# Attention and SwiGLU kernel on one core: last block product in its own bank, another order of one-pair products, weight sums stored later and made sooner

## The chip, the cores and the metric

One Trainium2 chip, one core. The metric is the device time of one execution in microseconds (us); lower is better. A core has a matrix engine (TensorE, PE in the profile), a vector engine (VectorE, DVE), a scalar engine (ScalarE, ACT), GpSimd (POOL) and SyncE (SP), which here only issues DMAs. PE writes its results to PSUM, here eight banks of 128 x 512 float32; the other data lies in SBUF.

## The reference

Normed attention for 8 sequences, 12 heads, 448 tokens, head size 64; its output, 3584 x 768, goes through a feed-forward block with 1536 hidden units. All float32.

```python
q_n, k_n = rmsnorm(q, g_q), rmsnorm(k, g_k)
attn = softmax(q_n @ k_n.T / sqrt(64))
x = (attn @ v)  ->  (3584, 768)
xn = x / rms(x) * rms_g
g, val = xn @ w_gate, xn @ w_val            # 768 x 1536 each
out = (g * sigmoid(g) * val) @ w_out        # 1536 x 768
```

## The kernel before, in words

The program is laid out by hand: one Python function emits every instruction in a fixed order, and each engine works through its own list. `safe_scores` (the only part that runs on these inputs) goes through 48 pairs of heads. In between it pops items from a list `todo`: the gate and value products and the output products of the sequence before. A step is one call of `pe(fn)`; `now["t"]` counts them, and `after(n, fn)` emits `fn` n steps later.

**Products with fewer multiplications.** From sequence 1 on, gate and value use 15 products of block sums (`PRODUCTS`, `three`, `product`, matmuls on line 1408). The output product is a 2 x 2 block scheme with seven products, named after their right factors: B11, B21, T1 to T4, B22. The left factors are blocks A11 to A22 of the hidden values (tiles `h`) or their sums S1 to S4 (tiles `raw`). Three kinds of outputs:
- sequences 1 and 4, and 0 in plain form: `out_strassen` (matmuls on line 1681), two pairs of 128-row tiles for sequence 1, one pair for sequence 4. Each product takes two steps of three matmuls. B21 adds onto the bank of B11 and B22 onto that of T1, so the reader of the first must be done before the second starts. `ORDER_O` is the order.
- sequences 2, 3, 5, 6 and 7: `out_quads`, four tiles at once, where each of the seven products is itself split in the same way. `kept_q` holds the right factors of that second level. For each product i the steps are `a(i)`, `d(i-1)`, `bb(i)`, `c(i)`: a, b and c take two of the seven small products each, d the seventh, which adds onto c's bank. Matmuls on line 1752, left sums (tiles `l` and `raw`) on line 1626, DVE reads of the banks on lines 1772 to 1801; `finish` adds the results up on POOL (line 1723), for the last product on DVE (line 1743), and has `store` write them out (line 1578).

PE's results for this part go through three PSUM banks (`ps_f`), used in turn; scores use four others (`ps_s`).

**Weights.** All right factors lie in DRAM scratch (`kept`, `kept_o`, `kept_q`) and are streamed into an SBUF arena. `ask` (line 1287) issues a load as soon as the arena has a free place, in the order of use (`uses`); `used` gives a place back. All of it goes through SP's queue, together with the attention's inputs and the outputs.

**Weight sums for kept_q.** While sequence 1's outputs and sequence 2's gate and value products run, `derive_q` makes the second-level right factors: 21 jobs, each with two blocks x and y loaded from `kept_o` (line 1267), four DVE operations (lines 1371 to 1374) into two fresh places ta and tb, and four stores to `kept_q` (lines 1378 and 1381): a half of x, y, ta and tb. Two of these need no sum. `fill` calls `derive_q` after each step outside attention. A product of sequence 2's outputs may be loaded only when its three jobs are stored (`sums_q`).

Of the kernel before, what the change touches and what calls it, by code (L numbers as in the profile page):

```python
# [335 lines left out]
def safe_scores(  # L336
# [42 lines left out]
    def after(n, fn):  # L379
        due.append((now["t"] + n, fn))  # L380
# [562 lines left out]
    def norm_x(b):  # L943
# [293 lines left out]
    for b in range(1, B):  # L1237
        for n, g in enumerate(GROUPS):
            for at, name in enumerate(FIRST_RAWS if b == 1 else [right for _, _, right in PRODUCTS]):
                uses.append(("wg", b, g, name))  # L1240
        if in_quads(b):
            uses += stream_q(b)
        else:
            for name in ORDER_O:
                for c in range(NFP):
                    uses.append(("wo", b, name, c))
# [107 lines left out]
    todo_q = list(jobs_q)  # L1354

    def derive_q(wait=5):

        if not todo_q or sums_o or now["t"] - asked.get("at_q", 0) < 3 or asked["n"] in next_gate or not room(2, "wg"):
            return False
# [15 lines left out]

        def store():
            parts = kept_q[i].rearrange("p (n w) -> p n w", w=HW)
            nc.sync.dma_start(out=parts[:, j], in_=x[:, 0])
            for src, first, second in ((y, 1, 6), (ta, 2, 3), (tb, 4, 5)):
                gap = (second - first) * KG  # L1380
                nc.sync.dma_start(out=parts[:, first * KG + j:second * KG + j + 1:gap], in_=src)
# [181 lines left out]

    def store(b, n, i, y):
        row0 = at = b * S + i * 128 - 64 * (b % 2)
        while at < row0 + 128:
# [9 lines left out]
            else:  # L1576
                rows = out[rows + col:rows + col + m, cols]
            nc.sync.dma_start(out=rows, in_=y[at - row0:at - row0 + m, :])
            at += m
# [50 lines left out]
    def out_strassen(b):  # L1630
# [58 lines left out]
        pairs = out_pairs(b)  # L1689
        for name in ORDER_O:  # L1690
            for which in range(len(pairs)):
                for half in range(2):
                    steps.append(lambda a=(name, which, half, which == len(pairs) - 1): step(*a))
        return steps

    def out_quads(b):

        bank, dst, steps = {}, {}, []
        tiles = [i for pair in out_pairs(b) for i in pair]
        left = {}  # L1700
# [20 lines left out]
        def add(to, one, other):  # L1721
            for row in range(2):
                nc.gpsimd.tensor_tensor(to[row], one[row], other[row], ALU.add)  # L1723
# [50 lines left out]
        def bb(i):  # L1774
# [4 lines left out]
            nc.vector.tensor_tensor(u[:, 1], ps[:, 1], u[:, 0], ALU.add)  # L1779
            st["no_x"] = now["t"]  # L1780
            left_q1(b, i, (3,))
            if i == 0 or i > 1 and i + 1 < len(ORDER_Q):
                left_q1(b, i + 1, (0,))

        def c(i):
            ps = two(i, "c")
            st["heavy"] = now["t"]
            u3 = st["u", b, i][:, 1:2].to_broadcast([128, 2, HW])
            nc.vector.tensor_tensor(dst[i][1].rearrange("p (h n) -> p h n", h=2), ps, u3, ALU.add)
# [62 lines left out]
    def out_items(b):  # L1852
        if in_quads(b):
            return [(cost, TURNS, 0, fn) for cost, fn in out_quads(b)]
        if b >= FIRST_O:
            return [(NFP // 2 * HALF, TURNS, (0, ("wo", b, name, 3 * half + 2) if i == 0 else None), fn)
                    for (name, i, half), fn in zip(((name, i, half) for name in ORDER_O for i in range(len(out_pairs(b)))
                                                    for half in range(2)), out_strassen(b))]
# [180 lines left out]
    for g in range(NG + 1):  # L2039
# [62 lines left out]
        else:  # L2102
# [92 lines left out]
```

## Time and profile before

| | |
|---|---|
| median of 3 runs | 1487.42 us (1486.82 to 1487.74) |
| the profiled execution, own time | 1486.21 us |
| its span, first to last instruction | 1484.4 us |
| mean granted clock of TensorE | 0.997 |
| PE busy | 1456.5 us (98%) |
| DVE, ACT, POOL busy | 72%, 42%, 51% |
| last matmul ends | 1476.53 us |
| DMA queue of SP | 72.4% of 16 engines' span, 320.58 MB |

How to read it: times in the timeline are microseconds from the start of the span. A row is start, length, engine, line, operation, output <- inputs, shape and count; brackets give the idle time ahead of it and what ended it. SPq is SP's list of DMA issues. One fp32 matmul of the program shows as two in the trace, so a product of six shows x12.

### The profile page before, as it was taken

The numbers are of one execution on the slowest core, as the hardware profiler recorded it, in microseconds if no ns is written. First come the engines' busy times: TensorE is split into PE (matmuls) and PEld (weight loads), VectorE is DVE, ScalarE is ACT, GpSimd is POOL, SyncE is SP. The second block draws the span as 40 slices with busy tenths as digits, with TensorE's granted clock in tenths as the row PEclk, the third lists the DMA queues.
The fourth block names the chain that finished last, engine by engine and source line by source line (L and its number), as shares of the span: only waits on it lengthen the run. The fifth ranks groups of instructions, "written<-read, shape, count | busy, mean of one in ns | idle before, by whom it ended". The sixth has DMA issues, their size and how long they took to land.

```text
span 1484.4 us, 25739 instructions
## 1 busy us (share of the span) xinstructions
PE 1456.5 (98%) x8538; PEld 1141.9 (77%) x8538; DVE 1071.3 (72%) x1866; ACT 619.5 (42%) x1551; POOL 764.4 (51%) x684
## 2 busy tenths in 40 slices
PE   8999999999999999999999999999999999999997
PEld 4344444678855788888888889859898799899997
DVE  6788999699874677874579855755679756774664
ACT  7856776445523444234433443444542533101200
POOL 6877987647353363463545744645645842130002
PEclk9999999999999999999999999999999999999999
DMA  8758686676877899987566966677467855597675
GB/s 215 226 156 252 180 242 179 209 245 219 264 226 223 263 310 314 297 283 208 141 170 194 280 178 184 183 212 210 128 188 230 270 171 149 163 307 234 172 226 193
DMA packets 340577, 322.52 MB, mean 217 GB/s; under 512 B 126932, under 2 KB 282068, under 8 KB 340436
## 3 DMA queue, kind: packets, MB, share of 16 engines
q1 hardware_dynamic: 339508, 320.58, 72.4%
q8 instruction: 71, 1.16, 0.3%
q14 instruction: 70, 0.57, 0.1%
q10 hardware_dynamic: 800, 0.20, 0.1%
q0 software_dynamic: 128, 0.00, 0.0%
HBM read 266.90 MB, written 53.77 MB: 216 GB/s over the span
## 4 chain that ended last, share of the span: by engine, by line
PE 82%; DVE 11%; DMA 3%; issue 2%; SPq 1%; ACT 0%; POOL 0%; DVEq 0%; ACTq 0%; POOLq 0%
PE ff L1408 36%; PE ff L1752 13%; PE sc L805 8%; PE ff L1826 6%; PE av L823 6%; PE ff L1681 6%; PE ff L1551 2%; DMA w<-kept 2%; PE sc L705 1%; PE av L732 1%; PE den L749 1%; PE tr L684 1%; PE den L887 1%; DVE l L1626 1%; DVE x L959 1%
## 5 line engine op out<-in xcount | busy, mean ns | idle before, releaser
L909 POOL TENSOR_TENSOR es<-es,e 128x448 f32<-128x448 f32 x205 | 255.1, 1245 | 13.6
L1408 PE MATMUL ff<-x,w 128*128 128x224 f32 x1296 | 258.1, 353 | 0.3 <-DVE pc L1429 0.3
L1408 PEld LDWEIGHTS ff<-x,w 128*128 128x128 f32 x1296 | 243.6, 190 | 3.5 <-issue 2.1
L805 PE MATMUL sc<-qT,kT 64*64 64x448 f32 x1176 | 231.1, 539 | 0.0
L823 PE MATMUL av<-e,yard 64*64 64x448 f32 x1148 | 223.8, 538 | 0.0
L1408 PE MATMUL ff<-xs,w 128*128 128x224 f32 x832 | 164.7, 353 | 3.8 <-DMA w<-kept 3.1
L1408 PEld LDWEIGHTS ff<-xs,w 128*128 128x128 f32 x832 | 156.1, 190 | 7.7 <-issue 3.9
L805 PEld LDWEIGHTS sc<-qT,kT 64*64 64x64 f32 x1176 | 78.8, 133 | 86.1 <-issue 54.8
L786 POOL TENSOR_TENSOR ss<-ss,rd 128x448 f32<-128x448 f32 x40 | 47.6, 1191 | 159.4 <-ACT rd L785 158.0
L1752 PE MATMUL ff<-w,l 128*128 128x192 f32 x630 | 117.2, 329 | 4.5 <-DVE l L1626 2.2
L1429 DVE TENSOR_TENSOR pc<-ff,l 128x448 f32<-128x448 f32 x56 | 34.9, 622 | 108.6 <-PE ff L1408 77.8
L1826 PE MATMUL ff<-x,w 128*128 128x448 f32 x288 | 111.8, 541 | 0.0
L1752 PEld LDWEIGHTS ff<-w,l 128*128 128x128 f32 x630 | 103.8, 190 | 10.0 <-DVE l L1626 3.0
L823 PEld LDWEIGHTS av<-e,yard 64*64 64x64 f32 x1148 | 77.3, 133 | 36.9 <-issue 36.7
L904 POOL TENSOR_TENSOR es<-e 128x448 f32<-128x448 f32 x41 | 48.5, 1182 | 110.2 <-ACT e L813 79.9
L813 ACT ACTIVATE e<-sc 128x448 f32<-128x448 f32 x168 | 88.0, 547 | 36.5 <-PE sc L805 27.1
L1826 PEld LDWEIGHTS ff<-x,w 128*128 128x128 f32 x288 | 53.3, 190 | 51.1 <-issue 48.0
L811 ACT ACTIVATE e<-sc,yard 128x448 f32<-128x448 f32 x126 | 78.2, 634 | 32.7 <-PE sc L805 24.2
L1408 PE MATMUL ff<-top_x,w 128*128 128x224 f32 x440 | 91.1, 356 | 0.0
L1408 PEld LDWEIGHTS ff<-top_x,w 128*128 128x128 f32 x440 | 81.8, 190 | 11.5 <-issue 10.6
L1426 DVE TENSOR_TENSOR pb<-ff,pb 128x448 f32<-128x448 f32 x84 | 52.3, 622 | 47.8 <-PE ff L1408 47.7
L1723 POOL TENSOR_TENSOR y<-y,pa 128x384 f32<-128x384 f32 x10 | 11.1, 1127 | 144.6 <-DVE y L1801 137.2
(244 smaller groups left out, 2972.4 us busy)
## 6 DMA issues: line engine op xcount, KB each, us to landing
w<-kept SPq DMA_DIRECT2D x380, 256.0 KB, 3.9
w<-kept_q SPq DMA_DIRECT2D x350, 192.0 KB, 3.8
w<-kept_o SPq DMA_DIRECT2D x150, 192.0 KB, 3.8
kept_q<-w SPq DMA_DIRECT2D x63, 192.0 KB, 3.6
raw<-in_moe_w_gate_dram SPq DMA_DIRECT2D x24, 384.0 KB, 4.7
raw<-in_moe_w_val_dram SPq DMA_DIRECT2D x24, 384.0 KB, 4.2
kept<-w SPq DMA_DIRECT2D x48, 192.0 KB, 4.3
raw<-in_moe_w_out_dram SPq DMA_DIRECT2D x24, 384.0 KB, 3.7
```

The lines of the kernel that those rows point to most:

```text
L786: after(m, lambda: (nc.gpsimd.tensor_tensor(ss, ss, rd, ALU.add), st.update({("summed", b): hp})))
L805: nc.tensor.matmul(ps[r, 0:S], lhsT=keys(g, r, i), rhs=st["qT", g][r, :], start=True, stop=True)
L811: nc.scalar.activation(e, ps[:, 0:S], ACT.Exp, scale=st["rs", g][:, NB + i:NB + i + 1])
L813: nc.scalar.activation(e, ps[:, 0:S], ACT.Exp)
L823: nc.tensor.matmul(st["av", g][own(j), 0:S], lhsT=vt, rhs=st["e", g, i][r], start=i == 0, stop=i == PARTS - 1, skip_group_check=True)
L904: nc.gpsimd.tensor_tensor(st["es", g], st["e", g, 0], st["e", g, 1], ALU.add)
L909: nc.gpsimd.tensor_tensor(st["es", g], st["es", g], st["e", g, i], ALU.add)
L1408: nc.tensor.matmul(bank[:, w * HT:(w + 1) * HT], lhsT=data(key)[:, (2 * w + c) * 128:(2 * w + c + 1) * 128], rhs=a[left][:, c, :], start=o ...
L1426: nc.vector.tensor_tensor(T[name], ps[:, 0:S], T[name], ALU.add)
L1681: nc.tensor.matmul(ps, lhsT=left_o(b, which, LEFT_O[name], c), rhs=data(("wo", b, name, c)), start=first and c == 0, stop=c == NFP - 1, sk ...
L1752: nc.tensor.matmul(ps, lhsT=a[:, j, :], rhs=data(key)[:, n % 2 * HW:(n % 2 + 1) * HW], start=start and j == 0, stop=j == KG - 1, skip_grou ...
L1826: nc.tensor.matmul(bank[w][:, 0:S], lhsT=data(key)[:, c * 128:(c + 1) * 128], rhs=st["x", 0][:, 3 * half + c, :], start=half == c == 0, st ...
```

## The change

1. `norm_x`: the broadcast of the row scales of sequence 1 (`rb`) uses a bank of `ps_s` instead of `ps_f`.
2. `order_o`: outputs with one pair (sequence 4) run in the order B11, T2, B21, T3, T1, T4, B22 instead of B11, B21, T2, T3, T1, B22, T4. The weights are loaded in that order too.
3. `derive_q`: until the loads reach the first gate products of sequence 2, the fresh places are taken from the other end of the arena and a job may follow after 4 steps instead of 3; around the first seven of those loads jobs are allowed if three places are free, where none were before. The half of x and y are stored at once, ta and tb 3 steps later (before: all four 1 step later). ta, tb and y's places are given back 6 steps after the job (before: 7 for ta and tb, from the second product on). `derive_q` is also called once inside each attention block.
4. `out_quads` for the last sequence: the seventh small product of the last block product gets its own bank. Its left sum is made a product earlier. T1's result is added into tiles pb and pc by POOL row by row, and B22's small products are added to pb on the way, so no full-tile addition is left behind the last matmul; the two stores of the last tile go through SP's and ACT's queues.

The core of the diff:

```diff
-            ps = (ps_s if b > 1 else ps_f).tile([128, 512], F32, name="rb", tag="s" if b > 1 else "f")
+            ps = (ps_s if b else ps_f).tile([128, 512], F32, name="rb", tag="s" if b else "f")
...
     ORDER_O = ("B11", "B21", "T2", "T3", "T1", "B22", "T4")
+    def order_o(b):
+        return ORDER_O if len(out_pairs(b)) > 1 else ORDER
...
+    def own_kind():
+        return "w" if asked["n"] <= next_gate[0] else "wg"
     def derive_q(wait=5):
-        if not todo_q or sums_o or now["t"] - asked.get("at_q", 0) < 3 or asked["n"] in next_gate or not room(2, "wg"):
+        if not todo_q or sums_o or now["t"] - asked.get("at_q", 0) < (4 if asked["n"] <= next_gate[0] else 3) or asked["n"] in next_gate and not room(3, "wg") or not room(2, own_kind()):
             return False
...
-        st[own_a], st[own_b] = block("wg"), block("wg")
+        st[own_a], st[own_b] = block(own_kind()), block(own_kind())
...
-        def store():
-            parts = kept_q[i].rearrange("p (n w) -> p n w", w=HW)
-            nc.sync.dma_start(out=parts[:, j], in_=x[:, 0])
-            for src, first, second in ((y, 1, 6), (ta, 2, 3), (tb, 4, 5)):
-                gap = (second - first) * KG
-                nc.sync.dma_start(out=parts[:, first * KG + j:second * KG + j + 1:gap], in_=src)
+        def store(src, first, second):
+            gap = (second - first) * KG
+            nc.sync.dma_start(out=parts[:, first * KG + j:second * KG + j + 1:gap], in_=src)
+        def store_sums():
+            store(ta, 2, 3)
+            store(tb, 4, 5)
             asked["sums_q"] = asked.get("sums_q", 0) + 1
-        after(1, store)
+        nc.sync.dma_start(out=parts[:, j], in_=x[:, 0])
+        store(y, 1, 6)
+        after(3, store_sums)
         for key in (*keys, own_a, own_b):
-            after(7 if i and key[0] != "wx" else 4, lambda key=key: used(key))
+            after(6 if key[0] != "wx" else 4, lambda key=key: used(key))
...
+        end = len(ORDER_Q) - 1 if b == B - 1 else None
...
+        def split_sum(row):
+            m = dst[end - 1][row]
+            nc.gpsimd.tensor_tensor(dst[2][row], dst[2][row], m, ALU.add)
+            nc.gpsimd.tensor_tensor(dst[3][row], dst[3][row], m, ALU.add)
+            after(1, lambda: store(b, 1, tiles[2 + row], dst[3][row]))
         def finish(i):
-            if name == "B21":
+            if end and i == end - 1:
+                split_sum(0)
+                left_q1(b, end, (3,))
+                half = lo_hi(dst[end][0])[0]
+                nc.vector.tensor_tensor(half, half, lo_hi(dst[2][0])[0], ALU.add)
+            elif end and i == end:
+                store(b, 1, tiles[0], m[0], (nc.sync, nc.scalar))
+            elif name == "B21":
...
         def bb(i):
+            if end and i == end:
+                nc.vector.tensor_tensor(u[:, 0], u[:, 0], lo_hi(dst[2][0])[1], ALU.add)
+                both = dst[2][1].rearrange("p (h n) -> p h n", h=2)
+                nc.vector.tensor_tensor(both, both, u[:, 1:2].to_broadcast([128, 2, HW]), ALU.add)
+                return
...
         def c(i):
+            if end and i == end:
+                half = st["u", b, i][:, 0]
+                nc.vector.tensor_tensor(half, ps[:, 1], half, ALU.add)
+                nc.vector.tensor_tensor(dst[i][1].rearrange("p (h n) -> p h n", h=2), ps, dst[2][1].rearrange("p (h n) -> p h n", h=2), ALU.add)
+                store(b, 1, tiles[1], dst[i][1])
+                return
...
+            if end and i == end - 1:
+                split_sum(1)
         def d(i):
-            ps = bank[i, "c"]
-            term(i, 6, ps[:, 1], start=False)
+            if end and i == end:
+                ps = ps_f.tile([128, 512], F32, name="ff", tag="f")[:, 0:BW].rearrange("p (h n) -> p h n", h=2)
+            else:
+                ps = bank[i, "c"]
+            term(i, 6, ps[:, 1], start=bool(end) and i == end)
...
             pe(lambda: [step(g, i) for i in (1, 2)])
+            derive_q()
             pe(lambda: [step(g, i) for i in (3, 4)])
```

**SP's queue in the gate and value products of sequence 2, second group.** `w<-kept` loads a right factor, `w<-kept_o` a block for a later sum, `kept_q<-w` stores a part of a job. Before:

```order
L1287 DMA w<-kept 128x512
L1378 DMA kept_q<-w 128x192
L1381 DMA kept_q<-w 128x2x192 x3
L1287 DMA w<-kept 128x512
L1267 DMA w<-kept_o 128x384 x2
L1287 DMA w<-kept 128x512 x3
```

After, at the same place:

```order
L1290 DMA w<-kept 128x512
L1393 DMA kept_q<-w 128x192
L1386 DMA kept_q<-w 128x2x192
L1290 DMA w<-kept 128x512
L1270 DMA w<-kept_o 128x384 x2
L1386 DMA kept_q<-w 128x2x192 x2
L1290 DMA w<-kept 128x512 x4
```

The stores of ta and tb have moved behind one load of a right factor and two of blocks, and stand now directly ahead of the next right factors.

**PE in the outputs of sequence 4, between its first two attention blocks.** `h_115` to `h_118` are the hidden values (A11 and A12, or A22), `raw` the sums S2, S1 and S4. Before, from the second half of B21 on:

```order
L1681 MATMUL ff<-w,h_118 128x384 x3
L1681 MATMUL ff<-w,raw 128x384 x6
L1681 MATMUL ff<-w,h_115 128x384 x3
L1681 MATMUL ff<-w,h_116 128x384 x3
L1681 MATMUL ff<-w,raw 128x384 x12
L1681 MATMUL ff<-w,h_117 128x384 x3
```

After, from the second half of T2 on:

```order
L1693 MATMUL ff<-w,raw 128x384 x3
L1693 MATMUL ff<-w,h_117 128x384 x3
L1693 MATMUL ff<-w,h_118 128x384 x3
L1693 MATMUL ff<-w,h_115 128x384 x3
L1693 MATMUL ff<-w,h_116 128x384 x3
L1693 MATMUL ff<-w,raw 128x384 x6
L1693 MATMUL ff<-w,h_117 128x384 x3
L1693 MATMUL ff<-w,h_118 128x384 x3
L1693 MATMUL ff<-w,raw 128x384 x3
```

T2 stands ahead of B21, and T1 and B22, twelve matmuls in a row before, have T4 between them.

**DVE at the end.** Rows behind the last bank read of T1 (`pa`), up to the last one before the flag. `l` is a left sum, `th` a scratch tile, `ff` a bank, `y` an output tile. Before:

```order
L1801 TENSOR_TENSOR pa<-ff,th 128x192
L1778 TENSOR_TENSOR th<-ff,th 128x192
L1779 TENSOR_TENSOR th<-ff,th 128x192
L1626 TENSOR_TENSOR l_12385<-raw,l_12350 128x384
L1789 TENSOR_TENSOR y<-ff,th 128x384
L1801 TENSOR_TENSOR y<-ff,th 128x192
L1743 TENSOR_TENSOR y<-y,pa 128x384 x2
```

After:

```order
L1844 TENSOR_TENSOR pa<-ff,th 128x192
L1638 TENSOR_TENSOR l_12374<-raw,l_12350 128x384
L1750 TENSOR_TENSOR y<-y,pb 128x192
L1804 TENSOR_TENSOR th<-ff,th 128x192
L1805 TENSOR_TENSOR th<-ff,th 128x192
L1808 TENSOR_TENSOR th<-th,pb 128x192
L1810 TENSOR_TENSOR pb<-pb,th 128x384
L1821 TENSOR_TENSOR th<-ff,th 128x192
L1822 TENSOR_TENSOR y<-ff,pb 128x384
L1844 TENSOR_TENSOR y<-ff,th 128x192
```

The left sum has moved ahead of the reads of b's bank, the additions of T1's result stand ahead of the last three bank reads, and the last row is a bank read of 192 columns.

More of the change, by code (lines that the diff above doesn't have):

```diff
@@ L1243, in safe_scores @@
         else:
-            for name in ORDER_O:
+            for name in order_o(b):
                 for c in range(NFP):
@@ L1374, in derive_q @@
         nc.vector.tensor_tensor(tb[:, 0], y[:, 0], ta[:, 0], ALU.subtract)
-        def store():
-            parts = kept_q[i].rearrange("p (n w) -> p n w", w=HW)
-            nc.sync.dma_start(out=parts[:, j], in_=x[:, 0])
-            for src, first, second in ((y, 1, 6), (ta, 2, 3), (tb, 4, 5)):
-                gap = (second - first) * KG
-                nc.sync.dma_start(out=parts[:, first * KG + j:second * KG + j + 1:gap], in_=src)
+        parts = kept_q[i].rearrange("p (n w) -> p n w", w=HW)
+        def store(src, first, second):
[4 more added lines that the diff above has]
+            store(tb, 4, 5)
             asked["sums_q"] = asked.get("sums_q", 0) + 1
-        after(1, store)
+        nc.sync.dma_start(out=parts[:, j], in_=x[:, 0])
+        store(y, 1, 6)
+        after(3, store_sums)
         for key in (*keys, own_a, own_b):
-            after(7 if i and key[0] != "wx" else 4, lambda key=key: used(key))
+            after(6 if key[0] != "wx" else 4, lambda key=key: used(key))
         return True
@@ L1562, in project_out, with store @@
         store(b, n, i, y)
-    def store(b, n, i, y):
+    def store(b, n, i, y, queues=(nc.sync, nc.sync)):
+        queues = list(queues)
         row0 = at = b * S + i * 128 - 64 * (b % 2)
@@ L1577, in store @@
                 rows = out[rows + col:rows + col + m, cols]
-            nc.sync.dma_start(out=rows, in_=y[at - row0:at - row0 + m, :])
+            queues.pop(0).dma_start(out=rows, in_=y[at - row0:at - row0 + m, :])
             at += m
@@ L1689, in out_strassen @@
         pairs = out_pairs(b)
-        for name in ORDER_O:
+        for name in order_o(b):
             for which in range(len(pairs)):
@@ L1787, in c @@
             st["heavy"] = now["t"]
+            if end and i == end:
+                half = st["u", b, i][:, 0]
+                nc.vector.tensor_tensor(half, ps[:, 1], half, ALU.add)
+                nc.vector.tensor_tensor(dst[i][1].rearrange("p (h n) -> p h n", h=2), ps,
+                                        dst[2][1].rearrange("p (h n) -> p h n", h=2), ALU.add)
+                store(b, 1, tiles[1], dst[i][1])
+                return
             u3 = st["u", b, i][:, 1:2].to_broadcast([128, 2, HW])
@@ L1856, in out_items @@
             return [(NFP // 2 * HALF, TURNS, (0, ("wo", b, name, 3 * half + 2) if i == 0 else None), fn)
-                    for (name, i, half), fn in zip(((name, i, half) for name in ORDER_O for i in range(len(out_pairs(b)))
+                    for (name, i, half), fn in zip(((name, i, half) for name in order_o(b) for i in range(len(out_pairs(b)))
                                                     for half in range(2)), out_strassen(b))]
```

## The prediction

> **What bounds the kernel now.** I read the page first, then TensorE's (PE's) list of waits, then the places of those waits in the timeline, then the last 15 us.
>
> ```profile
> span 1484.4 us, 25739 instructions
> PE 1456.5 (98%) x8538; PEld 1141.9 (77%) x8538; DVE 1071.3 (72%) x1866; ACT 619.5 (42%) x1551; POOL 764.4 (51%) x684
> ```
>
> PE is busy for 1456.5 of 1484.4 us, so 27.9 us are idle. The change adds and removes no matmul, so it can win idle time and the stretch behind the last matmul, nothing else. The list of waits says which idle time the change can reach:
>
> ```profile
> PE ff L1408 <- DMA w<-kept: 3.1, 3, 1.8
> PE ff L1408 <- DVE pb L1426: 2.4, 4, 1.1
> ...
> PE ff L1752 <- DMA w<-kept_q: 1.0, 1, 1.0
> ...
> PE ff L1752 <- DVE y L1789: 0.7, 1, 0.7
> PE ff L1681 <- DVE y L1653: 0.7, 1, 0.7
> ...
> PE ff L1681 <- ACT pa L1660: 0.6, 1, 0.6
> ```
>
> Each row gives the total, the times and the longest wait. The first and the third row and one wait of the second belong to the stage in which the weight sums are made, the fourth row to the end, the last two to the one-pair outputs of sequence 4.
>
> **Weight sums (derive_q).** These are the five waits in that stage, in PE's timeline; the idle time ahead of the row stands in brackets:
>
> ```profile
> 510.36 1.75 PE L1408 MATMUL ff<-xs,w 128*128 128x224 f32 x8 [1.80 <-DMA w<-kept]
> 543.47 1.75 PE L1408 MATMUL ff<-xs,w 128*128 128x224 f32 x8 [0.50 <-DMA w<-kept]
> 573.59 1.75 PE L1408 MATMUL ff<-xs,w 128*128 128x224 f32 x8 [0.79 <-DMA w<-kept]
> 599.17 1.02 PE L1408 MATMUL ff<-raw,w 128*128 128x224 f32 x4 [0.81 <-DVE pb L1426]
> 607.52 0.92 PE L1752 MATMUL ff<-w,l 128*128 128x192 f32 x4 [0.96 <-DMA w<-kept_q]
> ```
>
> Together 4.86 us. The loads come late because they share SP's queue with the stores of the sums, and those wait for VectorE (DVE):
>
> ```profile
> SPq L1381 <- DVE w L1374: 24.4, 14, 5.1
> ...
> 501.30 2.23 SPq L1381 DMA_DIRECT2D kept_q<-w  x3
> ...
> 505.13 1.33 SPq L1287 DMA_DIRECT2D w<-kept  x3
> ...
> 566.55 3.97 SPq L1381 DMA_DIRECT2D kept_q<-w  x3
> ...
> 502.17 0.97 DVE L1374 TENSOR_TENSOR w<-w 128x192 f32<-128x192 f32 x1
> ```
>
> Three issues take 1.33, one 0.44; what the L1381 rows have above that, 0.9 and 2.6 us, is waiting with the loads queued behind. After the change the two stores that need no sum go out at once, and the two of sums three steps later instead of one; the number of DMAs is the same. At 510.36 (right factor b12 of the second group) the new order puts the stores of the sums right ahead of the load: they can go when L1374 ends at 503.14, take 0.9, so the load is issued near 504.1 instead of 505.13: 1.0 of the 1.80 goes. At 543.47 the queue ahead of the load is as long as before: 0.2 of 0.50. At 573.59 the load now stands ahead of the sums' stores, and the 2.6 us of waiting in front of it leave: all 0.79.
>
> The other two waits come from the last three of the 21 sums. The code's own step counter puts them at steps 366, 371 and 374 before and the last one at 357 after, so 12 DVE operations leave the stretch from 592 to 603 us. The first four took 3.16 us (592.17 to 595.33):
>
> ```profile
> 592.17 1.28 DVE L1371 TENSOR_TENSOR w<-w 128x192 f32<-128x192 f32 x1
> ...
> 594.97 0.36 DVE L1374 TENSOR_TENSOR w<-w 128x192 f32<-128x192 f32 x1
> ```
>
> That is more than the 0.81 that PE waited at 599.17, so this wait goes; and the loads of kept_q that were asked for 2 to 4 steps ahead of their use now get 7 to 12, so the 0.96 goes. Sum: 1.0 + 0.2 + 0.8 + 0.8 + 1.0 = **3.8 us**. Ends: all five go (4.86), or only the last two and half of the rest's 2.0 (2.8); worse is a rival below. The sums made instead during the outputs of sequence 1 cost nothing there: PE's timeline shows no wait between 408 and 476 us, and a bank comes back into use only two products of 4.0 us (the row at 980.65 below) after its own.
>
> The extra call of derive_q inside an attention block catches one sum. Four DVE operations at 0.35 to 1.28 us, 1.4 to 4.8 us together, stand ahead of the multiplication that frees the av bank, whose next user comes behind at least two products: nothing. If that cover is gone, PE waits for up to the remainder, under 2 us.
>
> **One-pair outputs (sequence 4).** Before, B21 adds to B11's bank right behind B11 and must wait until ACT has copied it; B22 adds to T1's bank right behind T1 and waits for DVE:
>
> ```profile
> 963.32 2.20 PE L1681 MATMUL ff<-w,h 128*128 128x384 f32 x6 [0.57 <-ACT pa L1660]
> 980.65 4.03 PE L1681 MATMUL ff<-w,raw 128*128 128x384 f32 x12
> 985.34 4.14 PE L1681 MATMUL ff<-w,raw 128*128 128x384 f32 x12 [0.65 <-DVE y L1653]
> ```
>
> Now T2 (row like 980.65, 4.0 us in another bank) stands between the first two and T4 between the second two; the readers need 0.5 us. Both waits go: **1.2 us**. T2 starts with the half of S2 that was made a stage earlier, so nothing new is late; if it were, the same 0.6 would come back.
>
> **The end (sequence 7, last product).** Timeline, engines mixed:
>
> ```profile
> 1466.51 0.55 DVE L1626 TENSOR_TENSOR l<-raw,l 128x384 f32<-128x384 f32 x1
> 1471.22 1.95 POOL L1723 TENSOR_TENSOR pc<-pc,pa 128x384 f32<-128x384 f32 x2 [4.88 <-DVE pa L1801]
> 1473.34 1.21 DVE L1626 TENSOR_TENSOR l<-raw,l 128x384 f32<-128x384 f32 x1
> 1473.44 1.14 PE L1752 MATMUL ff<-w,l 128*128 128x192 f32 x6
> 1474.67 0.56 DVE L1789 TENSOR_TENSOR y<-ff,th 128x384 f32<-128x384 f32 x1
> 1475.29 1.24 PE L1752 MATMUL ff<-w,l 128*128 128x192 f32 x6 [0.71 <-DVE y L1789]
> 1476.57 0.36 DVE L1801 TENSOR_TENSOR y<-ff,th 128x192 f32<-128x192 f32 x1 [1.34 <-PE ff L1752]
> 1477.03 1.03 DVE L1743 TENSOR_TENSOR y<-y,pa 128x384 f32<-128x384 f32 x2
> 1477.62 1.80 SPq L1578 DMA_DIRECT2D out_dram<-y  x3
> ```
>
> Before, the last six matmuls wait 0.71 for DVE to read the shared bank; then come 0.36 and 1.03 of DVE and three issues, ending at 1479.42. After, on the same clock: PE goes on at 1474.41 and ends near 1475.55. POOL gives the first row of pb near 1472.2 (half of 1.95 from 1471.22). DVE then has 0.36, twice 0.36, 0.36 and 0.55: done near 1474.4. Behind c's products (1474.58) it has 0.36 and 0.56, to 1475.6, and behind d's 0.36, to 1476.0. SP issues one store from 1475.6 and a half one from 1476.2, ending near 1476.75: 2.67 earlier.
>
> Is SP's end what counts?
>
> ```profile
> L2165 SPq EVENT_SEMAPHORE  x8: 17/17/17, 1482.3 to 1482.8; - x8
> ...
> L2165 ACTq EVENT_SEMAPHORE  x1: 17/17/17, 1473.2 to 1473.2; - x1
> ...
> L2164 ACTq TENSOR_LOAD <-flag x1: 480/480/480, 1469.8 to 1469.8; - x1
> ...
> 0.73 1.38 ACTq L560 DMA_DIRECT2D yard<-in_q_dram  x2
> ...
> DMA to landing us min/median/max: 2.2/2.3/2.5
> ```
>
> SP's last issue ends at 1479.42 and its last event is at 1482.8, 3.4 later; the span ends 1.6 behind that. The stores land 2.2 to 2.5 us after their issue (last row), which is sooner. ACT needs 3.4 us from its flag load to its event, and an issue on it takes 0.69 (1.38 for two). Its new half store goes from 1476.05 to 1476.74, so its event is near 1480.15; SP's, 3.4 behind 1476.75, as well. The end moves from 1482.8 to 1480.15, by 2.65. If DVE's operations with two SBUF inputs each lose a POOL operation, as at 1473.34 (1.21 for the 0.55 of 1466.51, so 0.66 more), and one such loss reaches the chain, it is 2.0. I take **2.5 us**, near the free case, since DVE has 0.2 us to spare ahead of c and the last three operations read PSUM.
>
> The Trainium skill, "SBUF — State Buffer", section "Who interferes with whom", says that a VectorE instruction with two SBUF inputs contends with a GpSimd instruction that reads SBUF, and that whoever comes second is blocked for the whole instruction. The row at 1473.34 agrees (1.21 against 0.55). By that rule at its worst two of POOL's operations are waited out whole, the sums ahead of c are ready near 1475.75 instead of 1474.4, and the end would win 1.6 instead of 2.5, which stays inside the forecast's own range.
>
> **rb in ps_s for sequence 1:** nothing. PE's timeline has no wait between 239 and 327 us, so none can go; a late bank could cost about what the longest wait on one does in the list, 0.7 us (L1789).
>
> **Sum.** 3.8 + 1.2 + 2.5 = 7.5 us. The profiled execution took 1486.21 (span 1484.4 and 1.8 around it), so 1478.7 by its own clock; it lies 1.21 below the median of the runs, 1487.42, so the forecast in those terms is 1479.9, with a range of its own from 1478.0 (4.86 + 1.2 + 2.65 = 8.7, and 0.7 of spread) to 1482.0 (2.8 + 1.2 + 2.0 = 6.0, less 0.6).
>
> **Rivals.**
> - *The queue stays the limit.* If SP's issue rate (near 567 us some ten issues of 0.44 us to three products of 1.75 us) and not the waiting makes the loads late, and DVE is late at 599 for its other work, the first stage gives 0 to 1.5: 1482.0 to 1484.3. For it: 543.47, whose queue is as long as before. Against it: 2.6 us of pure waiting at 566.55.
> - *The end is held by something else*, such as the reused y tile, whose previous store now stands behind one that waits for POOL: POOL starts on it at 1468.4, behind the first row below, and needs two operations of 0.98; the store goes near 1470.8, lands 2.5 us later, 1473.3, and is needed at 1475.0. It has 1.7 us to spare; if it failed, 1 to 2.5 us less, 1480.9 to 1482.4, within the other ranges.
> - *Slower: places.* Made sooner, the sums take places in the weight arena during the outputs of sequence 1, so eight later loads are asked for 6 to 8 steps ahead instead of 9 to 12. A load that comes late has cost up to 1.80 (510.36). At that price eight cost 14.4 against the 7.5: 1494.3. It decides once a lead of 6 steps, 12 us at half of 4.03 a step, is shorter than the way from issue to use, 5.1 us for the load of 505.13; it is twice as long, so I give it little.
>
> The rows for the last two, from the timeline and from the chain of work (start, length):
>
> ```profile
> 1467.79 0.56 DVE L1789 TENSOR_TENSOR pa<-ff,th 128x384 f32<-128x384 f32 x1 [0.26 <-PE ff L1752]
> ...
> 505.13 5.10 DMA w<-kept
> ```
>
> - *No effect:* new waits of the size of the old ones appear one step later: 1484.5 to 1490.4.
>
> **Chances.** Forecast 0.68; queue the limit 0.15; better than 1478.0 (waits that follow from these go too) 0.04; no effect 0.08; slower 0.05. A measurement of this kernel can tell about 0.2%, 3.0 us, from no change. So faster by more than that (below 1484.4): 0.87; within it 0.08; slower 0.05. The range reaches from 1477.2, the forecast's low end with some of the better case, to 1484.3, the end of the first rival.
>
> **What would show it.** Right: in the profile after, PE's waits for y L1653, pa L1660 and y L1789 are gone; no wait for w<-kept_q; w<-kept down to about 1 us; SP's wait on L1374 well below 24.4; the stretch from the last matmul to the end of the span 6.2 us instead of 7.9. Wrong: new PE waits for DMA between 408 and 520 us, SP still waiting over 10 us for the sums, or DVE operations of 1.2 us in the last 5 us.

## The result, and the profile after

| | before | after |
|---|---|---|
| median of 6 runs each, same chip | 1486.76 us (1484.12 to 1487.74) | 1475.10 us (1473.55 to 1476.27) |
| ratio, 95% interval | | 0.9924 [0.9911, 0.9936] |
| the profiled execution, own time | 1486.21 us | 1474.93 us |
| its span | 1484.4 us | 1473.1 us |
| PE idle in the span | 27.9 us | 19.2 us |

The forecast was 1479.9 us with a range from 1477.2 to 1484.3; the measured median lies below the range. The gain is 11.7 us by the medians and 11.3 by the spans, where 7.5 were forecast. The page of after:

```profile
span 1473.1 us, 25744 instructions
PE 1453.9 (99%) x8538; PEld 1142.2 (78%) x8538; DVE 1073.0 (73%) x1868; ACT 620.1 (42%) x1551; POOL 763.9 (52%) x684
```

PE has as many instructions as before, yet its busy time fell by 2.6 us. No term of the forecast can do that, since none removes a matmul: some of the same matmuls have become quicker (1.8 us of it will be found at `rb`, some 0.5 at the order). PE's list of waits after (total, times, longest):

```profile
PE ff L1778 <- DVE l L1638: 2.2, 2, 1.2
PE ff L1419 <- DMA w<-kept: 1.9, 2, 1.0
PE ff L1419 <- DVE pb L1437: 1.6, 3, 1.1
...
PE sc L805 <- DVE x L959: 0.5, 1, 0.5
```

The counterparts of all rows that the forecast named are gone (kept_q, y L1653, pa L1660, y L1789), or smaller (w<-kept 3.1 to 1.9, pb 2.4 to 1.6). A row has come, sc L805, for which the forecast had a price (a late bank, 0.7 us at most) but no place. And one more row is gone. It stood third in the list of before, with the longest single wait, and the forecast didn't quote it:

```profile
PE ff L1551 <- DVE h L1835: 2.4, 1, 2.4
```

Its place is found in PE's timeline of before (start, length, and in brackets the idle time ahead):

```profile
236.40 0.55 PE L953 MATMUL rb<-ident,rs 112*128 112x112 f32 x4
239.30 9.70 PE L1551 MATMUL ff<-w,h 128*128 128x384 f32 x24 [2.36 <-DVE h L1835]
248.93 0.59 PE L805 MATMUL sc<-qT,kT 64*64 64x448 f32 x2
```

The same place in the timeline of after:

```profile
236.04 0.55 PE L953 MATMUL rb<-ident,rs 112*128 112x112 f32 x4
236.43 7.92 PE L1562 MATMUL ff<-w,h 128*128 128x384 f32 x24
244.28 0.59 PE L805 MATMUL sc<-qT,kT 64*64 64x448 f32 x2
...
247.27 0.59 PE L805 MATMUL sc<-qT,kT 64*64 64x448 f32 x2 [0.51 <-DVE x L959]
```

`rb` for sequence 1 is written at 236.40 and held until DVE has scaled x with it, behind 247. Before, it took one of the three banks of `ps_f`. The next product (outputs of sequence 0) found the other two still occupied by the plain gate and value products, and waited until DVE's row L1835 had read one:

```profile
238.63 0.61 DVE L1835 SCALAR_TENSOR_TENSOR h<-th,ff 128x448 f32<-128x448 f32 x1
```

This row ends at 239.24, PE starts at 239.30. After, `rb` sits in a score bank: the wait is gone, and the first score that wants that bank waits 0.51 us instead. Besides, the 24 matmuls behind the wait took 9.70 us before and take 7.92 after. That is the clock. The windows of before (stretch, share of each engine, and third from the right the granted clock):

```profile
239.00:240.00 1.00, 0.70 (x2) 0.49 (x3) 0.93 (x4) 0.00 (x0) 1.00 (x1) 1.00 0.85 298
240.00:241.00 1.00, 1.00 (x4) 0.51 (x3) 1.00 (x3) 0.00 (x0) 0.92 (x3) 0.76 0.51 191
241.00:242.00 1.00, 1.00 (x3) 0.55 (x2) 0.97 (x3) 0.00 (x0) 1.00 (x2) 0.50 0.00 0
242.00:243.00 1.00, 1.00 (x3) 0.54 (x2) 0.97 (x2) 0.55 (x2) 1.00 (x2) 0.50 0.00 0
243.00:244.00 1.00, 1.00 (x2) 0.47 (x2) 1.00 (x2) 0.46 (x2) 1.00 (x2) 0.54 0.86 89
244.00:245.00 1.00, 1.00 (x5) 0.60 (x4) 1.00 (x2) 0.00 (x0) 1.00 (x2) 1.00 0.60 201
```

The clock falls to half at about 240.5 and is back at about 243.9. For those 3.4 us PE does half of its work: 1.7 us lost, which the list of waits doesn't show, since PE counts as busy. Not every execution loses it, as e1 will show.

**Where the 11.3 us went.** The span can be cut at rows that both traces have: the start of `rb` (L953); the wait of 1.12 us for pb near 402 us; the wait of 0.51 us for pa near 651; the first product of sequence 4's outputs; the denominators (den L887) near 982; the last twelve matmuls with `raw` near the end; the end of the last matmul; the end of the span. Lengths in us:

| stage | before | after | gain | forecast |
|---|---|---|---|---|
| start to rb | 236.40 | 236.04 | 0.36 | 0 |
| rb to 402 (rb's bank) | 170.16 | 166.58 | **3.58** | **0** |
| 402 to 651 (weight sums) | 251.67 | 248.42 | 3.25 | 3.8 |
| 651 to sequence 4's outputs | 300.49 | 300.48 | 0.01 | 0 |
| their products to den (order) | 32.62 | 30.87 | 1.75 | 1.2 |
| den to the last product | 480.15 | 480.16 | 0 | 0 |
| last product to last matmul (own bank) | 5.04 | 4.06 | 0.98 | 2.5, with the next |
| last matmul to the end | 7.87 | 6.49 | 1.38 | |

Three of the four terms came out within 0.6 us each and add up to 7.4. The fourth, put at nothing, brought 3.6. The two stages in the middle that the change doesn't touch repeat to 0.02 us, so a cut of this kind can show far smaller effects than a comparison of whole times. Not every stage is so steady: the start, untouched too, lies between 236.04 and 236.40 us in all the profiles of this study, so its 0.36 isn't a gain of the change.

### The profile page after: what moved, and what is told of

Its sections match the earlier page's. It is cut to its first block, busy times and chain, and to the rows that moved or that the text cites. A ratio compares the mean times of both kernels' runs of the same rounds, so it can differ in the third digit from the quotient of the medians.

```text
span 1473.1 us, 25744 instructions
## 1 busy us (share of the span) xinstructions
PE 1453.9 (99%) x8538; PEld 1142.2 (78%) x8538; DVE 1073.0 (73%) x1868; ACT 620.1 (42%) x1551; POOL 763.9 (52%) x684
## 4 chain that ended last, share of the span: by engine, by line
## 5 line engine op out<-in xcount | busy, mean ns | idle before, releaser
L805 PE MATMUL sc<-qT,kT 64*64 64x448 f32 x1176 | 231.5, 539 | 0.6 <-DVE x L959 0.5
L805 PEld LDWEIGHTS sc<-qT,kT 64*64 64x64 f32 x1176 | 78.8, 133 | 87.2 <-issue 53.8
```

The source lines that it names most:

```text
L805: nc.tensor.matmul(ps[r, 0:S], lhsT=keys(g, r, i), rhs=st["qT", g][r, :], start=True, stop=True)
```

## Experiments

Each kernel is made from before or after by one edit (e12 by none) and was run in five rounds beside before. There were three groups, each on a chip of its own: e1 to e4, then e5, e6, e7 and e9, then e8, e10, e11 and e12. The median of before in them was 1486.29, 1486.21 and 1486.78 us, so a difference between groups is good to 0.6 us at best. The lengths of the same stages from each kernel's own profile:

| kernel | median, us | rb | sums | order | own bank | end |
|---|---|---|---|---|---|---|
| before | 1486.8 | 170.16 | 251.67 | 32.62 | 5.04 | 7.87 |
| before, rb in ps_s (e2) | 1482.51 | 166.56 | 252.38 | 32.62 | 5.04 | 7.73 |
| before, rb wait filled (e3) | 1484.85 | 168.44 | 252.12 | 32.62 | 5.03 | 7.80 |
| before, rb wait filled in part (e10) | 1486.43 | 168.45 | 251.66 | 32.62 | 5.04 | 7.81 |
| before, own bank (e7) | 1485.40 | 170.09 | 252.14 | 32.62 | 4.36 | 7.94 |
| after, first runs | 1475.10 | 166.58 | 248.42 | 30.87 | 4.06 | 6.49 |
| after, again (e12) | 1474.90 | 166.61 | 248.09 | 30.87 | 4.06 | 6.56 |
| after, rb in ps_f (e1) | 1477.40 | 170.12 | 249.61 | 30.86 | 4.06 | 6.90 |
| after, old order (e4) | 1477.25 | 166.60 | 249.09 | 32.62 | 4.06 | 6.42 |
| after, old derive_q (e5) | 1479.26 | 166.58 | 252.98 | 30.87 | 4.06 | 6.80 |
| after, old end (e6) | 1478.42 | 166.61 | 248.78 | 30.87 | 5.03 | 8.41 |
| after, rb copied (e8) | 1475.29 | 165.85 | 248.58 | 30.87 | 4.06 | 7.14 |
| after, sums stored later (e9) | 1476.62 | 166.57 | 248.50 | 30.87 | 4.06 | 6.60 |
| after, left sums split (e11) | 1474.39 | 166.61 | 249.98 | 30.87 | 4.06 | 6.56 |

### rb back in its old bank (e1), and rb alone (e2)

```diff
# e1, from after; e2 is the reverse edit, from before
-            ps = (ps_s if b else ps_f).tile([128, 512], F32, name="rb", tag="s" if b else "f")
+            ps = (ps_s if b > 1 else ps_f).tile([128, 512], F32, name="rb", tag="s" if b > 1 else "f")
```

> The changed kernel with one edit undone: the broadcast rb of sequence 1 takes a bank of ps_f again. Theory A (the bank that rb holds makes PE wait 2.4 us at the plain output product, and the clock that falls to a half after that wait costs 1.7 more): the wait for DVE h comes back at 2.3 to 2.4 us, the granted clock has a stretch at 0.5 right behind it, the 0.5 us wait for DVE x goes, and the span grows by 3.2 to 3.9 us over the changed kernel's. Rival B (the 3.8 us that the forecast missed lie elsewhere, in the weight sums or the start): the span changes by under 1 us.

> The kernel before with this one edit alone: rb of sequence 1 in ps_s. Theory A: the 2.36 us wait goes, no stretch at half clock behind it, a new wait of about 0.5 us of a score for DVE x appears in the next attention block; 3.2 to 3.9 us faster than the kernel before, ratio 0.9974 to 0.9978. Rival B: within 1 us of the kernel before.

e2: 1482.51 us (1481.68 to 1484.97, 11 runs), ratio 0.9978 [0.9969, 0.9987], 3.8 us below before. Its timeline at the place has no wait and the quick matmuls:

```profile
236.16 0.55 PE L953 MATMUL rb<-ident,rs 112*128 112x112 f32 x4
236.55 7.92 PE L1551 MATMUL ff<-w,h 128*128 128x384 f32 x24
```

e1: 1477.40 us (1476.34 to 1480.18), ratio 0.9941 [0.9928, 0.9955]. Its rb stage is as long as that of before, 170.12; its windows show the clock at 0.50 from 240 to 243 us, and the wait for sc L805 is gone. In these profiles one line of the program carries the 3.6 us, alone and within the change. By the median e1 loses only 2.3 us. Its profile is that of its slowest run (1480.18 us, mean granted clock 0.998). Its fastest run, 1476.34 us, has a mean clock of 1.000, and 3.4 us at half speed would alone bring it down to 0.9988: in that run the clock didn't fall. So the clock's 1.7 us are lost only in some executions.

### The wait filled with matmuls (e3, e10)

```diff
# from before, in norm_x behind the transposes to rb; e3 has warm(10), e10 warm(2)
+            if b == 1:
+                warm(10)
```

The added products of `ident` with itself go to a bank that nobody reads; the wait for the bank stays.

> The kernel before, rb still in ps_f, with ten matmuls of 128x128 without use (bank of ps_m, nobody reads it) behind the four transposes of rb, so that PE works through most of the wait. It parts the two halves of theory A. If the half clock comes from PE's idle time: the wait for DVE h shrinks to under 0.5 us, the granted clock stays at 1.0 behind it, the output product of 24 matmuls takes about 7.9 instead of 9.7 us, and the span is 1.5 to 2.0 us shorter than before. If the half clock has another cause: the stretch at 0.5 stays and the span changes by under 0.5 us.

> The kernel before with rb in its old bank and only two products of nothing (half a us) ahead of the wait, which leaves PE idle for some 1.9 us instead of 2.36. Theory A (the clock falls when enough of a stretch is idle, and 2.36 us is just above the point): clock 1.0 behind the gap, the 24 matmuls in 8.0 us, 1484.6 to 1485.0 us. Rival B (any gap much longer than 1 us at this place does it): clock 0.5 for 3.4 us behind the gap, 9.7 us for the 24 matmuls, 1486.3 us.

The timeline of e3 shows the wait filled and the 24 matmuls at full speed:

```profile
236.75 2.41 PE L1997 MATMUL warm<-ident 128*128 128x128 f32 x20
239.28 8.01 PE L1553 MATMUL ff<-w,h 128*128 128x384 f32 x24
```

So does that of e10, with 1.90 us of idle time left:

```profile
236.67 0.62 PE L1997 MATMUL warm<-ident 128*128 128x128 f32 x4
239.19 8.01 PE L1553 MATMUL ff<-w,h 128*128 128x384 f32 x24 [1.90 <-DVE h L1837]
```

In both the granted clock stays at 1.00 from 239 to 245 us. This splits the 3.58: 170.16 to 168.44 is the clock, 1.7 us; 168.44 to 166.58 is the wait, 1.9 us, which is 2.36 less the new 0.51. e3's median, 1484.85 (ratio 0.9992 [0.9983, 1.0001]), is 1.4 below before; that agrees with the 1.7 us, but its interval takes in no change. e10's median is 1486.43 (1.0002 [0.9993, 1.0011]), no better than before: its profiled run was the fastest of eleven. In some of the others the clock may have fallen: the mean granted clock is 0.996 or 0.997 in five of them (1486.24 to 1488.18 us), and 0.998 or 0.999 in all eleven runs of e3. This mean also takes in a fall behind the last matmul, so it doesn't settle the case. That 1.90 us are short enough always is therefore not shown.

### The old order for sequence 4 (e4)

```diff
-        return ORDER_O if len(out_pairs(b)) > 1 else ORDER
+        return ORDER_O
```

> The changed kernel with sequence 4's output products in the old order B11, B21, T2, T3, T1, B22, T4. The waits for ACT pa (0.57) and DVE y (0.65) come back, and PE needs 1.2 (the waits alone, the forecast's term) to 1.8 us more (with the start behind each wait, as the two traces show) for the stretch from the first output product to the next gate product. Rival: under 0.5 us, if the old waits are taken up elsewhere later.

1477.25 us (1476.78 to 1477.27), ratio 0.9939 [0.9926, 0.9953], 2.2 to 2.4 above after. In its list of waits the two rows are back:

```profile
PE ff L1693 <- DVE y L1665: 0.7, 1, 0.7
PE ff L1693 <- ACT pa L1672: 0.6, 1, 0.6
```

and the stage is 32.62 us long again, 1.75 more than after. The two waits have 0.57 and 0.65 us of idle time, 1.22 together; the other 0.53 is what stopping costs. In after's timeline a row follows the one ahead without a wait:

```profile
951.52 4.03 PE L1693 MATMUL ff<-w,h 128*128 128x384 f32 x12
955.39 2.10 PE L1693 MATMUL ff<-w,raw 128*128 128x384 f32 x6
```

It starts 0.16 us before the end of that row (951.52 and 4.03 make 955.55), and the six matmuls take 2.10 us where they took 2.20 behind the wait (963.32 of before). So a wait costs 0.16 and 0.10 beyond its idle time, 0.26 each.

### The old weight sums (e5), and the sums stored later still (e9)

```diff
# e9, from after; e5 has the whole derive_q of before, and no call inside attention
-        after(3, store_sums)
+        after(5, store_sums)
-            after(6 if key[0] != "wx" else 4, lambda key=key: used(key))
+            after(8 if key[0] != "wx" else 4, lambda key=key: used(key))
```

> The kernel after with the whole old derive_q (four stores one step after the job, no extra call, old places). Theory A (the weight sums' part of the change is worth what the two traces show for the stage, 3.25 us): 1475.1 + 3.25 = 1478.4 us, PE's waits for w<-kept and kept_q back, SP's wait for the sums back above 20 us. Rival B (the stage became quicker because it starts at another moment, 3.9 us earlier, and not by the edit): 1475.1 us and SP's wait still near 11 us. The forecast's own term, 3.8 us, would give 1478.9.

> The kernel after with the sums stored five steps behind the job instead of three, places given back after eight instead of six. Theory A (the stores of sums, waiting on DVE in SP's queue, still hold up the loads behind the two waits of 0.97 us for w<-kept): both waits shrink, 1472.9 to 1474.5 us, SP's wait for the sums below 6 us. Rival B (the queue's length, not its waiting, makes these loads late): both waits stay, 1475.1 us. Rival C (places given back two steps later delay other loads): 1476 to 1480 us with new waits for w<-kept.

e5: 1479.26 us (1476.88 to 1481.95), ratio 0.9954 [0.9940, 0.9967], 4.2 above after; its stage is 252.98, no shorter than the 251.7 to 252.4 of the other kernels with the old sums, though it starts 3.6 us earlier than that of before. PE's waits are back at the five places (1.37, 1.79, 1.56, 0.81 and 0.38 us). So it is the edit and not the moment. SP's wait for the sums fell from 24.4 us to this in after:

```profile
SPq L1386 <- DVE w L1380: 11.0, 9, 2.9
```

and it is 26.4 in e5. (In after 3.5 us more are put down to L1379, the operation before.) What is left in after are two waits in PE's timeline, the second longer than its counterpart before:

```profile
505.86 1.75 PE L1419 MATMUL ff<-xs,w 128*128 128x224 f32 x8 [0.97 <-DMA w<-kept]
...
539.26 0.99 PE L1419 MATMUL ff<-xs,w 128*128 128x224 f32 x4 [0.97 <-DMA w<-kept]
```

e9: 1476.62 us (1474.98 to 1478.15), ratio 0.9937 [0.9924, 0.9951], 1.5 above after by the median, with intervals that overlap. Its profile is that of the second fastest of its five runs. There the wait of the stores for L1380 is down to 2.2 us (4.3 more are put down to L1379), and still the stage is 248.50 us, with waits of 1.04 and 1.24 us at other places:

```profile
504.19 3.27 PE L1419 MATMUL ff<-xs,w 128*128 128x224 f32 x16 [1.04 <-DVE w L1380]
...
568.46 1.75 PE L1419 MATMUL ff<-xs,w 128*128 128x224 f32 x8 [1.24 <-DMA w<-kept]
```

So less waiting of the stores for DVE didn't shorten the stage, against theory A. The first of the two waits ends, by the profile, with an operation of DVE for a sum (L1380) and not with a load. Whether the number of issues in SP's queue or the places given back later make the waits, e9 doesn't separate, since it changes when stores go out and when places come back; its median is what the rival with the places had expected.

### The old end (e6), and the own bank alone (e7)

```diff
# e6, from after
-        end = len(ORDER_Q) - 1 if b == B - 1 else None
+        end = None
# e7, from before, in c(i) and d(i) of the last product
+                half = st["u", b, i][:, 0]
+                nc.vector.tensor_tensor(half, ps[:, 1], half, ALU.add)
...
-            ps = bank[i, "c"]
-            term(i, 6, ps[:, 1], start=False)
+                ps = ps_f.tile([128, 512], F32, name="ff", tag="f")[:, 0:BW].rearrange("p (h n) -> p h n", h=2)
+            term(i, 6, ps[:, 1], start=last)
```

> The kernel after with the old end of sequence 7 (shared bank, full-tile additions behind the last matmul, all stores on SP). Theory A (the end is worth 2.3 us by the traces, 2.5 by the forecast): 1477.4 us, the wait of 0.7 us for y L1789's counterpart back and 7.9 us from the last matmul to the end of the span. Rival B (the tail is set by what follows the last stores on SP and is the same in both): 1475.1 to 1475.8 us.

> The kernel before with the last small product in a bank of its own, and nothing else of the new end (one addition of 128x192 more, the c half into u, behind the c products). Theory A (the 0.71 us wait goes, and 0.15 to 0.25 us of restart with it): PE's part of the end gets 0.7 to 0.95 us shorter, 1485.3 to 1485.6 us, 7.9 us behind the last matmul as before. Rival B (the added addition and DVE's chain set the end): PE's wait goes, but the stretch behind the last matmul grows by as much: 1486.3 us.

e6: 1478.42 us (1477.94 to 1478.62), ratio 0.9948 [0.9935, 0.9962], 3.3 above after; its last two stages are 2.9 longer. e7: 1485.40 us (1483.09 to 1486.98), ratio 0.9995 [0.9986, 1.0004], not to be told from before by its time; by its profile the wait is gone and the last stage of PE is 0.68 shorter, which is the 0.71 of the wait. The new end as a whole takes 0.98 off this stage. The other 0.30 probably comes from the left sum that is made a product earlier: in e7 it still ends at 1474.64, 1.20 us long, and the last twelve matmuls take 2.41 us, where they take 2.11 in after. That part wasn't run by itself. The timeline of after at the end:

```profile
1463.41 1.00 POOL L1741 TENSOR_TENSOR pc<-pc,pa 128x384 f32<-128x384 f32 x1
1463.49 1.14 DVE L1750 TENSOR_TENSOR y<-y,pb 128x192 f32<-128x192 f32 x1 [0.89 <-POOL pb L1740]
...
1464.50 2.11 PE L1778 MATMUL ff<-w,l 128*128 128x192 f32 x12
...
1465.32 0.36 DVE L1808 TENSOR_TENSOR th<-th,pb 128x192 f32<-128x192 f32 x1
1465.59 0.55 DVE L1810 TENSOR_TENSOR pb<-pb,th 128x384 f32<-128x384 f32 x1
1466.06 0.35 DVE L1821 TENSOR_TENSOR th<-ff,th 128x192 f32<-128x192 f32 x1
1466.33 0.55 DVE L1822 TENSOR_TENSOR y<-ff,pb 128x384 f32<-128x384 f32 x1
1466.80 0.35 DVE L1844 TENSOR_TENSOR y<-ff,th 128x192 f32<-128x192 f32 x1
1466.90 0.91 SPq L1590 DMA_DIRECT2D out_dram<-y  x2
1467.17 0.57 ACTq L1590 DMA_DIRECT2D out_dram<-y  x1
```

The last matmul ends at 1466.61, DVE 0.5 us behind it, SP's last issue 1.2 behind it, and the span 5.3 behind that.

### Two tries to go further (e8, e11), and after once more (e12)

```diff
# e8, in norm_x
+        if b == 1:
+            held = ps
+            ps = tmp.tile([128, 2, S], F32, name="pc", tag="pc", bufs=1)[:, 0]
+            nc.scalar.copy(ps[:, 0:S], held[:, 0:S])
# e11, in left_sums, fill and bb(2): S3 and S4 go into a list of their own
-            first_sums.extend(ops)
+            first_sums.extend(ops[:2])
+            tail_sums.extend(ops[2:])
...
+            if i == 2:
+                hurry(tail_sums)
```

> The kernel after, unchanged, as the mark for the others of this group. Theory: 1473.6 to 1476.3 us as in its first six runs, its spread coming from the stage of the weight sums, whose PE waits for w<-kept differ from profile to profile (0 to 1 us at three or four places), and not from rb, the one-pair outputs or the end, which should repeat to 0.1 us.

> The kernel after with one more operation: ACT copies rb of sequence 1 from its score bank to SBUF, and the six scalings of x read the copy, so that the score bank comes free at once. Theory A: the new wait of 0.51 us for x L959 near 247 us goes, 0.5 to 0.75 us less than the kernel after. Rival B: the scalings, now with two SBUF inputs and POOL at work beside them, take longer than 0.6 us each and the left sums behind them come late: 0 to 2 us more than the kernel after.

> The kernel after, where in the outputs of four tiles the left sums S3 and S4 of the first level, which only later products read, are no longer all made ahead of the second-level sums of T2, but behind those of its last product. Theory A: four to five operations of 0.47 us leave the chain ahead of PE's two waits for l L1638 (1.22 us near 798 and 0.95 us near 1126), both go, and with some 0.25 us of restart for each the time is 2.2 to 2.7 us below the kernel after: 1472.5 us. Rival B: the sums moved behind make T3's left sums late instead, a wait of the same size one product later: 1475 us.

e12: 1474.90 us (1474.35 to 1475.52), ratio 0.9924 [0.9911, 0.9938]: the result repeats, rb's stage, the order's and PE's part of the end to 0.03 us, the sums' stage to 0.33.

e8: 1475.29 us (1474.83 to 1475.76). The wait for x L959 is gone and the rb stage 0.76 us shorter, as hoped; DVE pays for it, as the row of its timeline shows beside that of after (243.50, 3.63 us for the same six):

```profile
243.80 5.16 DVE L964 SCALAR_TENSOR_TENSOR x<-x,rg,pc 128x448 f32<-128x448 f32 x6
```

No new wait of PE came of it. The 0.76 doesn't show in the time: the tail behind the last matmul, 6.4 to 7.1 us in the kernels with the new end, varies by as much.

e11: 1474.39 us (1473.64 to 1475.51), 0.5 below e12, which the runs can't tell from nothing. The two waits for l L1638 (2.2 us) are gone, and two new ones have come one product later, as its rival said, but smaller:

```profile
PE ff L1779 <- DVE pc L1830: 1.3, 2, 0.7
```

Each of the two stages is 0.67 us shorter (299.81 for 300.48 and 479.49 for 480.16). This is the fastest kernel of the study by its median. What its profile shows as gained is the 1.3 us of these two stages; the stage of the sums, which varies from profile to profile, is 1.5 to 1.9 longer in it.

## Why the prediction was right in sign and wrong in size

- **The step that failed: "rb in ps_s for sequence 1: nothing. PE's timeline has no wait between 239 and 327 us, so none can go."** The timeline has one, 2.36 us, in brackets at 239.30. It was in the list of waits too, as the row L1551 <- h L1835, and the forecast passed over it: the rows that it quoted are those of L1408, L1681 and L1752, the lines that the other edits are about, and a bank that is taken away from one product is waited for by another product, on another line. Shown by e1 and e2: 3.6 us of stage in both, 3.8 us of time in e2 and 2.3 in e1, where the clock didn't fall in every run. The price given to it, at worst 0.7 us of loss for a late bank, was of the right size (0.51, sc L805) but is the smaller half of the exchange.
- **A wait was taken to cost its idle time.** At rb it cost 1.7 us more in the profile, because the clock fell behind it (e3). The Trainium skill, "TensorE: Matmul & The Clock Gate", section "The HAM clock gate", says that the clock goes to half rate after at least one idle window of about 3.4 us and comes back after a busy one. The 3.4 us at half rate agree with it; that 2.36 us of idle time suffice doesn't follow from it, and the measurement decides (last section).
- **Weight sums, 3.8.** Measured 3.25 in the first pair, and over all profiles 252.2 (mean of six with the old sums) to 248.9 (mean of seven with the new): 3.2. The three waits of 0.79, 0.81 and 0.96 went, as forecast; that of 1.80 fell to 0.97, where 0.80 was forecast; that of 0.50 was to fall to 0.3 and rose to 0.97. The queue ahead of that load was the doubt, and the first rival named it; that it is what holds this load up wasn't tested. Two of the forecast's own signs came out against it: SP's wait for the sums stayed above 10 us (11.0), and w<-kept fell to 1.9 us, not to about 1.
- **One-pair outputs, 1.2.** The mechanism was right (e4); the size is 1.75, since a wait costs some 0.26 us beyond its idle time.
- **The end, 2.5.** Measured 2.4 here, 2.9 by e6, whose tail is 0.5 longer than that of before with the same code. PE's part is 0.98, as worked out (1476.53 to 1475.55); SP's last issue ends 1.2 behind the last matmul, as worked out; the tail behind it is 5.3 us, where 5.0 was taken. DVE's addition of 192 columns beside POOL's, L1750 at 1463.49, took 1.14 us, where L1808 without POOL took 0.36; this used up the 0.2 us to spare and some 0.5 more ahead of c's last reads, and d's matmuls covered nearly all of it.
- **Slower by places: no.** No new wait for DMA came between 408 and 476 us.
- **The rest of the miss.** Of the 4.8 us between 1479.9 and 1475.1, 3.6 are rb and 0.4 the start, which is chance; 0.7 comes from the mark: the median of before was 1487.42 in three runs and is 1486.76 in six. The errors of the other three terms nearly cancel; that the sums' 0.55 too much and the order's 0.55 too little do so is luck.

## What to carry to other kernels

When a change moves a tile out of a pool, look for the waits of every other user of that pool, on any line; begin with the longest single wait of the list, not with the lines of the diff. Where such a wait is about 2 us or longer, read the granted clock just behind it: what follows may run at half speed, and counts as busy. And cut the span at rows that both traces share: the two untouched stages in the middle repeat to 0.04 us in all profiles but that of e11, where whole times spread over 3; the start, the tail and the stage of the sums vary by 0.4, 0.7 and more.

## What was not expected of the hardware

- An idle time of 2.36 us on PE was followed by 3.4 us at a granted clock of 0.5 in all three profiles that have it (before, e1, e7); waits of 1.79 and 1.80 us (e5, before) and 1.90 (e10) weren't, in one profile each. The fall doesn't come at a fixed distance. The idle time ends near 239.2 in all three; the clock fell at 240.5 in before and at 239.9 in e1, when PE was busy again, and at 238.9 in e7, while it still waited:

```profile
238.00:239.00 1.00, 0.00 (x0) 0.00 (x0) 1.00 (x3) 0.46 (x2) 1.00 (x1) 0.97 0.97 126
239.00:240.00 1.00, 0.97 (x2) 0.67 (x3) 0.93 (x3) 0.00 (x0) 1.00 (x1) 0.50 0.92 350
```

- The traces' records of the granted clock show what sets the moment. In all fourteen profiles the clock changes only a whole number of stretches of 3.413 us after the first record: the first time at full speed lasts 235.52 us in before and e1 (69 stretches), 232.11 in e7 (68) and 1464.32 in after (429). Where these stretches begin differs from execution to execution. Whether the clock falls goes with how long PE was busy in the stretch that has just ended, as the windows over single stretches show (the first number behind the comma is PE's busy time in us): in before, where the clock fell at the end, and in e10, where it didn't.

```profile
237.10:240.51 3.41, 1.21 (x4) 0.81 (x5) 3.27 (x9) 1.00 (x2) 3.23 (x3) 1.00 0.72 210
237.37:240.78 3.41, 1.59 (x5) 1.06 (x6) 3.27 (x8) 1.01 (x2) 3.25 (x4) 1.00 0.74 189
```

  In the fourteen profiles every full-speed stretch with at most 1.33 us of PE's work ended in a fall (1.33 is e7's at the last matmul, 1474.57 to 1477.98), and none with 1.59 us or more did. So a gap of 2.36 us that a stretch holds nearly whole lowers the clock, and one that is cut in two by the end of a stretch may not. The second half is inferred; it would explain e1's runs.
- From the last DMA issue to the end of the span pass 4.8 (e3) to 5.9 us (e8), whatever the end looks like; the tail behind the last matmul varies by some 0.7 us among kernels that are the same there.
